# A planned Trainium2 kernel whose scheduler now picks each tile's bank itself: six banks for the first group's first layer, another step pattern

## The chip, the core and the metric

The kernel runs on one core of a Trainium2 chip. The metric is the device time of one execution in microseconds (us), the median of repeated runs; lower is better.

## What is computed

Three layers follow each other: a chunked attention with decays, a block that takes the maximum of three products, and a block with a rational function. Cut to what matters:

```python
# attention: x (4, 8, 768, 32), B, C (4, 8, 768, 16), a (4, 8, 768); chunks of 32 in the reference
L = np.exp(cum[:, :, :, None] - cum[:, :, None, :]) * causal          # cum: cumsum of log(clip(a))
y = ((C @ B^T) * L) @ x + (C @ state) * np.exp(cum)[..., None]
state = decay_full * state + sum_j B_j x_j decay_from_j
x = y.transpose(0, 2, 1, 3).reshape(3072, 256)
# layer 1: d_ff = 768
x = np.maximum(np.maximum(x @ w1, x @ w2), x @ w3) @ w_out            # 256 -> 768 -> 256
# layer 2: d_ff = 2048
h = x @ w_in
P = a[0] + a[1] * h + a[2] * h**2 + a[3] * h**3
Q = 1.0 + abs(b[0]) * abs(h) + abs(b[1]) * h**2
out = (P / (Q + 1e-06)) @ w_out2                                      # 256 -> 2048 -> 256
```

The six weight matrices come as 64-bit floats and are converted on the chip.

## The kernel before

**Tiling.** The sequence is cut into six groups of 128 positions (`NG`), so that one group of all four batches is a tile of 512 columns (`T`). Every tile of work is 128 partitions by 512 columns, and one such tile in PSUM is one bank. All eight banks are in use: G, D, S0 to S3, Y0, Y1.

**Attention of a group**, in two halves of four units each: `s_mm` (L585) makes four products C B in S0 to S3 (L597); for each unit `d_mm` (L603) makes the exponent of the decays in one bank (L610, L612), ScalarE takes its exp (L625), and `m_op` (L627) multiplies it on VectorE with the S bank (L630), which frees that bank. `y_intra` (L642), `y_inter` (L653) and `state` (L677, then L687 and L694 on VectorE) do the rest; `y_out` (L657) copies the result out of Y0 and Y1. Group 0's result is split there into a high and a low part (float32r has too few bits for one product, so every product is three matmuls, L749 to L751: high by high, high by low, low by high). The results of groups 1 to 5 are stored in DRAM (`xt_d`) and loaded again by `x_plan` (L813).

**Weights.** `plan_conv` (L297) converts a piece of 128 x 512 weights: DMA (L323), ScalarE (L327, L330, and the high part L286), VectorE (L328, L331, L334), GpSimd (L339 and the low part L343, two halves each). There are 28 pieces: nine of w1 to w3, three of w_out, eight of w_in, eight of w_out2 (`wo2`). The last eight use SBUF places (L0 to L7) that attention leaves.

**Layer 1** of a group (`gy_plan`, L824): 18 products of six matmuls, drained by ScalarE (L286, w1) and VectorE (L840, the maximum with w2's and w3's), split (L386), then two products of 18 matmuls each with w_out. For group 0 `gy_bank` (L800) gives bank G alone to all 20 tiles (`EARLY`); for later groups G and D by turns.

**Layer 2** (`h_plan`, L875, and `o_plan`, L967): 16 steps per group. A step is a product of six matmuls into S0 or S1, the rational function on ScalarE, VectorE and GpSimd, and two accumulating products with wo2 into S2 and S3. How the numerator and denominator are shared out over the engines is the kind of the step, given by `HV` for groups 0 to 4: H is L922, L924 on ScalarE, L925 and L927 on GpSimd, L928 and L929 on VectorE; A is L932, L933, L943 on ScalarE, L934, L946 on VectorE, L945 on GpSimd; P is L932, L933 on ScalarE, L934, L939, L940 on VectorE and L937 on GpSimd. All kinds go on with L948 and L949 (ScalarE), L950, L953, L955 (VectorE), and the split of the result, L286 (ScalarE) and L961 (GpSimd). The last group has kinds of its own (`HL`) and no split.

**What sets the order.** Nothing is issued as it is written. `Plan.op` records each operation with its engine, an assumed duration, what it reads and writes and a due time (`when`, booked by hand through `book`); `Plan.emit` (L216) lists all operations with `listed`, a list scheduler with the planner's own durations, several times with changed keys, and issues the best order found. In the kernel before a tile's place (bank or SBUF buffer) is fixed when the operation is recorded: `bank("G")`, or `ring`, which hands out its places by turns, and a tile waits for the tile that had its place before:

```python
    def tile(self, place, make):
        t = _Tile(make, self.last.get(place, ()))
        self.last[place] = [t]
        return t
```

Of the kernel before, what the change touches and what calls it, by code (L numbers as in the profile page):

```python
# [34 lines left out]
EARLY = 20  # L35
PAIR = 1
HV, HL = "HAHP", "HHKK"
# [9 lines left out]
class _Tile:  # L47


    def __init__(self, make, prevs=()):  # L50
        self.make, self.prevs, self.t = make, prevs, None
        self.first, self.writers, self.readers, self.closed = None, [], [], False
# [44 lines left out]
class Plan:  # L97

    TAIL = {"pe": 0.22, "act": 0.13, "dve": 0.115, "pool": 0.07}
    SWITCH, FIRST_BYTE, LANDED, FLIGHTS, BEGIN = 0.1, 1.25, 1.35, 8, 0.65
    ROUNDS, LOOK, KEEP = 8, (0.0, 0.1, 0.2), (0.0, 1.5)

    def __init__(self):
        self.ops, self.last = [], {}
# [6 lines left out]
    def op(self, engine, busy, fn, reads=(), writes=(), at=None, behind=(), lock=False, mode="", size=0.0):  # L113
        i = len(self.ops)
        deps, after = set(), {w for t in behind for w in t.writers}
        for t in reads:
            assert t.writers and not t.closed
            deps.update(t.writers)
            t.readers.append(i)
        for t in writes:  # L120
            assert not t.closed
            if t.first is None:
                t.first = i
                for p in t.prevs:
                    p.closed = True
                    deps.update(p.writers + p.readers)
# [4 lines left out]
        self.ops.append(_Op(i, engine, busy, fn, [t for t in writes if t.first == i], deps, after - deps, at,  # L131
                            lock, mode, size))

    def listed(self, key, look, keep):
# [9 lines left out]
        moved, mode, landed, order = 0.0, "", [0.0] * self.FLIGHTS, []  # L144

        def at(j):
            t = self.BEGIN
            for i, _ in self.before[j]:
                if i in ops[j].after:
                    t = max(t, start[i])  # L150
                elif ops[i].engine == ops[j].engine != "dma":
                    t = max(t, start[i] + ops[i].busy)
                else:
                    t = max(t, end[i] + (0.05 if ops[j].engine == "pool" else 0.0))
            return t
# [5 lines left out]
        for _ in range(n):  # L161
            t, e = min((max(free[e], min(ready[j] for j in w)), e) for e, w in wait.items() if w)
# [915 lines left out]
```

## Time and profile before

| | |
|---|---|
| median of 3 runs | 569.52 us (569.35 to 569.66) |
| the profiled execution | 570.01 us, its span 568.2 us |
| TensorE (PE) busy | 546.7 us, 96% of the span |
| PE weight loads (PEld) busy | 411.8 us, 72% |
| VectorE (DVE) busy | 513.7 us, 90% |
| ScalarE (ACT) busy | 433.6 us, 76% |
| GpSimd (POOL) busy | 437.9 us, 77% |
| granted TensorE clock | 1.00 throughout |
| HBM traffic | 33.2 MB, nearly all in the first 140 us |

Matmuls are pipelined: a row of 0.39 us starts 0.23 us after the one before it. A busy share is an average over stages, so the windows by stage, further below, say more than this table. In a wait row the engine on the left sat idle until the one on the right had finished; the numbers are the sum, how often, and the longest.

### The profile page before, as it was taken

To read this page: it belongs to the slowest core of one execution; us is meant where nothing else is said; L and a number is where in the kernel's file an instruction comes from. 1 tells how busy PE (TensorE), PEld (TensorE's weight loads), DVE (VectorE), ACT (ScalarE), POOL (GpSimd) and SP (SyncE) were. 2 spreads that over 40 slices of the span, in tenths; PEclk is the share of its full clock that TensorE was granted. 3 is DMA by queue.
4 is the path that set the end of the run, shared out by engine and by line. 5 is a ranking of instruction groups with operands and counts; after the bars stand their busy time and mean duration, and the time that the engine had idled before them with its cause. 6 is when DMAs were issued, how large, how long until landed. Compare 5 with 4: busy or idle time off the path is not lost.

```text
span 568.2 us, 8235 instructions
## 1 busy us (share of the span) xinstructions
PE 546.7 (96%) x2844; PEld 411.8 (72%) x2854; DVE 513.7 (90%) x782; ACT 433.6 (76%) x756; POOL 437.9 (77%) x403
## 2 busy tenths in 40 slices
PE   9889889998999999999999999999999999999997
PEld 4455555567788888888887788878788888887563
DVE  7999899889999998988888987998889899988996
ACT  5767677779888877877787776868777877688983
POOL 1677677789899878777677685767777999879984
PEclk9999999999999999999999999999999999999999
DMA  7966575353000100001000010000000000001000
GB/s 246 311 208 195 179 246 189 118 204 122 1 0 2 37 2 37 1 0 39 0 1 37 1 37 1 1 37 2 0 1 1 1 37 1 0 1 37 2 0 37
DMA packets 13588, 33.71 MB, mean 59 GB/s; under 512 B 2691, under 2 KB 3435, under 8 KB 13547
## 3 DMA queue, kind: packets, MB, share of 16 engines
q1 hardware_dynamic: 13547, 33.20, 17.7%
q8 instruction: 22, 0.36, 0.3%
q14 instruction: 19, 0.16, 0.1%
HBM read 27.27 MB, written 5.91 MB: 58 GB/s over the span
## 4 chain that ended last, share of the span: by engine, by line
PE 42%; DVE 32%; POOL 12%; ACT 7%; issue 5%; DMA 1%; SPq 0%; POOLq 0%; DVEq 0%; ACTq 0%
PE S L750 6%; PE S L751 6%; PE S L749 6%; PE S L979 4%; PE G L749 4%; DVE X L840 4%; DVE Y L953 4%; PE G L751 3%; PE G L750 3%; DVE A L950 3%; DVE A L955 3%; PE D L749 3%; PE D L751 3%; PE D L750 3%; DVE A L630 2%
## 5 line engine op out<-in xcount | busy, mean ns | idle before, releaser
L961 POOL TENSOR_TENSOR A<-A,A 128x512 fp32r<-128x512 f32 x80 | 106.9, 1337 | 10.6 <-ACT A L286 10.3
L948 ACT ACTIVATE Y<-A,qc 128x512 f32<-128x512 f32 x83 | 57.7, 695 | 45.4 <-POOL A L927 30.0
L950 DVE SCALAR_TENSOR_TENSOR A<-A,Y 128x512 f32<-128x512 f32 x83 | 56.4, 680 | 8.2 <-ACT Y L949 7.9
L386 POOL TENSOR_TENSOR H<-X,H 128x512 fp32r<-128x512 f32 x30 | 41.6, 1388 | 27.4 <-ACT H L286 27.3
L749 PE MATMUL S<-A,L 128*128 128x512 f32 x160 | 62.3, 389 | 0.0
L750 PE MATMUL S<-A,L 128*128 128x512 f32 x160 | 62.3, 389 | 0.0
L751 PE MATMUL S<-A,L 128*128 128x512 f32 x160 | 62.3, 389 | 0.0
L339 POOL TENSOR_TENSOR C<-C,E 128x256 uint32<-128x256 uint32 x56 | 45.4, 825 | 21.8 <-DVE C L334 21.0
L953 DVE SCALAR_TENSOR_TENSOR Y<-A,co,Y 128x512 f32<-128x512 f32 x83 | 62.1, 748 | 0.0
L927 POOL TENSOR_TENSOR A<-A,A 128x512 f32<-128x512 f32 x44 | 57.8, 1314 | 3.6
L955 DVE SCALAR_TENSOR_TENSOR A<-A,Y 128x512 f32<-128x512 f32 x83 | 56.7, 683 | 1.3
L286 ACT ACTIVATE A<-A 128x512 fp32r<-128x512 f32 x80 | 50.4, 630 | 8.8 <-DVE A L955 7.4
L749 PE MATMUL G<-xhi,w_hi 128*128 128x512 f32 x126 | 51.7, 410 | 4.1 <-ACT X L286 2.0
L949 ACT ACTIVATE Y<-Y 128x512 f32<-128x512 f32 x86 | 50.3, 584 | 1.8
L751 PE MATMUL G<-xhi,w_lo 128*128 128x512 f32 x126 | 49.2, 391 | 0.0
L750 PE MATMUL G<-xlo,w_hi 128*128 128x512 f32 x126 | 49.2, 390 | 0.0
L925 POOL TENSOR_SCALAR A<-A,co 128x512 f32<-128x512 f32 x44 | 38.7, 880 | 8.1 <-ACT A L924 8.1
L922 ACT ACTIVATE A<-S,co 128x512 f32<-128x512 f32 x40 | 31.2, 780 | 16.3 <-POOL A L961 16.1
L945 POOL TENSOR_TENSOR A<-A,A 128x512 f32<-128x512 f32 x20 | 26.1, 1307 | 21.6 <-DVE A L934 19.7
L749 PE MATMUL D<-xhi,w_hi 128*128 128x512 f32 x90 | 35.6, 395 | 3.7 <-DVE X L840 3.7
L750 PE MATMUL S<-K,win_hi 128*128 128x512 f32 x96 | 37.5, 390 | 0.4 <-DVE K L386 0.4
L749 PE MATMUL S<-K,win_hi 128*128 128x512 f32 x96 | 37.5, 390 | 0.0
(192 smaller groups left out, 1651.8 us busy)
## 6 DMA issues: line engine op xcount, KB each, us to landing
R<-in_wo_dram SPq DMA_DIRECT2D x11, 512.0 KB
R<-in_w_dram SPq DMA_DIRECT2D x9, 512.0 KB
R<-in_win_dram SPq DMA_DIRECT2D x8, 512.0 KB
L<-in_xn_dram SPq DMA_DIRECT2D x6, 512.0 KB
out_dram<-A SPq DMA_DIRECT2D x12, 256.0 KB
xt_d<-L SPq DMA_DIRECT2D x5, 512.0 KB
L<-xt_d SPq DMA_DIRECT2D x5, 512.0 KB
A<-in_bz_dram SPq DMA_DIRECT2D x6, 256.0 KB
```

What stands on the lines that cost most here:

```text
L286: act.activation(out=o, in_=i, func=AF.Copy)
L339: op("pool", 0.7, lambda k=k: pool.tensor_tensor(out=a.t[:, k], in0=a.t[:, k], in1=e.t[:, k], op=ALU.add), [e], [a])
L749: pe.matmul(dst, wh, hi, start=first, stop=False)
L750: pe.matmul(dst, wh, lo, start=False, stop=False)
L751: pe.matmul(dst, wl, hi, start=False, stop=last)
L927: pop(1.26, lambda: pool.tensor_tensor(out=f(v), in0=f(t1), in1=f(v), op=ALU.mult), [t1], [v])
L948: aop(0.6, lambda: act.activation(out=f(r), in_=f(v), func=AF.Ln, bias=qc), [v], [r])
L949: aop(0.49, lambda: act.activation(out=f(r), in_=f(r), func=AF.Exp, scale=-1.0), [], [r])
L950: dop(0.6, lambda: dve.scalar_tensor_tensor(out=f(v), in0=f(v), scalar=QC, in1=f(r), op0=ALU.add, op1=ALU.mult), [r], [v])
L953: dop(0.67, lambda: dve.scalar_tensor_tensor(out=f(r), in0=f(w), scalar=c(0), in1=f(r), op0=ALU.add, op1=ALU.mult), [w], [r])
L955: dop(0.6, lambda: dve.scalar_tensor_tensor(out=f(w), in0=f(v), scalar=2.0, in1=f(r), op0=ALU.subtract, op1=ALU.mult), [v, r], [w])
L961: pop(1.26, lambda: pool.tensor_tensor(out=f(lo), in0=f(w), in1=f(hi).bitcast(F32), op=ALU.subtract), [w, hi], [lo])
```

## The change

Places are no longer given out when an operation is recorded. A tile carries a list of places that it may have, and `listed` gives it, at the moment at which its first writer is issued, the first of them that is free, or the one that will be free soonest (`spot`). Operations of one kind keep their order among themselves (`turn`). A tile marked `final` waits for all tiles that could have its place. On top of that:

- Decays (`d_mm`) may have D or G in all groups (before: G and D by turns in group 0, then D alone). Layer 1 of group 0 may have any of G, D, S0 to S3.
- The fourth step of `HV` is of kind H in place of P.
- Group 1's attention result stays in SBUF (`x1`): one store and one load of 512 KB go.
- In the last group the product of a step may have G, D, S0, S1 and its reciprocal Y0, Y1 (before: G, D, and S0, S1 or Y0, Y1).
- Products of layer 2 may not be issued before the last four L630 of attention have begun; `state` follows its group's exp. The planner's price of a change of TensorE's mode is 0.12 in place of 0.10, and decays count as a mode.

```diff
-EARLY = 20
-PAIR = 1
-HV, HL = "HAHP", "HHKK"
+SBANKS, DBANKS, FIRST_BANKS, GBANKS = (), ("D", "G"), ("G", "D", "S0", "S1", "S2", "S3"), ("G", "D")
+LAST, LAST_R = ("G", "D", "S0", "S1"), ("Y0", "Y1")
+HV, HL = "HAHH", "HHKK"
...
-    def tile(self, place, make):
-        t = _Tile(make, self.last.get(place, ()))
-        self.last[place] = [t]
+    def tile(self, places, make, final=False, kind=None):
+        t = _Tile(make, places, kind)
+        if final:
+            t.prevs = [p for p in self.tiles if places[0] in p.places] + self.fixed.get(places[0], [])
+        self.tiles.append(t)
         return t
...
+        for k in [turn] * bool(turn) + [t.kind for t in writes if t.first is None and len(t.places) > 1]:
+            if k in self.turns:
+                after.add(self.turns[k])
+            self.turns[k] = i
...
+        def spot(i):
+            t, got = ready[i], []
+            for x in ops[i].first:
+                best = None
+                for p in x.places:
+                    if not open_.get(p) and p not in got:
+                        u = behind(users.get(p, ()), i, 0.0)
+                        if best is None or u < best[0] - 1e-9:
+                            best = u, p
+                        if u <= t:
+                            break
+                if best is None:
+                    return None
+                t = max(t, best[0])
+                got.append(best[1])
+            return t, got
...
-        t = bank("G" if g < PAIR and d_n[0] % 2 else "D")
+        t = bank(*DBANKS, kind="d")
...
-        if g:
+        if g == 1:
+            x1.append(xo)
+        elif g:
             xt_t[g] = mark()
             load(lambda: xt_d[g], lambda: xo.t, [xt_t[g]], [xo], kb=524)
...
     def gy_bank(g):
-        banks[0] += 1
-        if g:
-            return pg()
-        return bank("G") if banks[0] <= EARLY else late()
+        return bank(*(GBANKS if g else FIRST_BANKS), kind="g")
...
-        t = pg() if last else ph()
+        t = bank(*(LAST if last else ("S0", "S1")))
...
-           when["h", s] + (0.5 * 6 * MM if c0 else 0))
+           when["h", s] + (0.5 * 6 * MM if c0 else 0), behind=[m_t[u] for u in range(NG * NU - 4, NG * NU)], turn="h")
...
-        r = ph() if last and (k + (c0 > 0)) % 3 else pr()
+        r = bank(*(LAST_R if last else ("Y0", "Y1")))
```

Three places show how the instructions stand now. Lines of the changed kernel are other ones: L703 is L630 of before, L909 is L840, L460 is L386, L406, L409 and L412 are L328, L331 and L334, L715 is L642, L824 to L826 are L749 to L751.

**VectorE in the middle of attention, around group 0's layer 1.** X0 and X1 are the running maxima, the second operand is the bank that is drained, S0 to S3 in L630 are attention's products. Before:

```order
L630 TENSOR_TENSOR A16_538<-S0_469,A10_533 128x512
L579 TENSOR_TENSOR A3_482<-A3_482,sm_94 128x512
L328 TENSOR_SCALAR C1_548<-C1_548 128x512
L840 TENSOR_TENSOR X0_453<-X0_453,G_540 128x512
L331 TENSOR_SCALAR C1_548<-C1_548 128x512
L334 SCALAR_TENSOR_TENSOR C1_548<-R2_362,C1_548 128x512
L630 TENSOR_TENSOR A17_585<-S1_470,A11_563 128x512
L386 TENSOR_TENSOR H6_599<-X0_453,H0_574 128x512
```

Now:

```order
L909 TENSOR_TENSOR X0_519<-X0_519,S0_618 128x512
L909 TENSOR_TENSOR X0_519<-X0_519,G_632 128x512
L703 TENSOR_TENSOR A15_699<-S3_555,A13_585 128x512
L909 TENSOR_TENSOR X1_671<-X1_671,S2_661 128x512
L460 TENSOR_TENSOR H6_708<-X0_519,H0_701 128x512
L406 TENSOR_SCALAR C1_705<-C1_705 128x512
L409 TENSOR_SCALAR C1_705<-C1_705 128x512
L412 SCALAR_TENSOR_TENSOR C1_705<-R1_544,C1_705 128x512
L909 TENSOR_TENSOR X1_671<-X1_671,S1_677 128x512
```

Before, one maximum out of G stands between attention's multiplications; now layer 1 of group 0 stands in one piece, out of six banks, between the fifth and the sixth half-group of attention, and no L630 stands among the following rows.

**VectorE at the end of attention**, from the last two L630 on. Before:

```order
L630 TENSOR_TENSOR A_1610<-S_1526,A_1595 128x512
L630 TENSOR_TENSOR A_1622<-S_1527,A_1614 128x512
L328 TENSOR_SCALAR C_1632<-C_1632 128x512
L331 TENSOR_SCALAR C_1632<-C_1632 128x512
L334 SCALAR_TENSOR_TENSOR C_1632<-R_1488,C_1632 128x512
L386 TENSOR_TENSOR K_1660<-G,K_1642 128x512
L386 TENSOR_TENSOR xlo_1676<-L_1612,xhi_1664 128x512
L386 TENSOR_TENSOR xlo_1682<-L_1612,xhi_1666 128x512
```

Now:

```order
L412 SCALAR_TENSOR_TENSOR C_1583<-R_1410,C_1583 128x512
L703 TENSOR_TENSOR A_1648<-S_1559,A_1596 128x512
L406 TENSOR_SCALAR C_1646<-C_1646 128x512
L409 TENSOR_SCALAR C_1646<-C_1646 128x512
L909 TENSOR_TENSOR X_1636<-X_1636,G 128x512
L412 SCALAR_TENSOR_TENSOR C_1646<-R_1476,C_1646 128x512
L997 TENSOR_TENSOR A_1683<-S_1658,A_1683 128x512
```

The splits of layer 1's result (K) and of group 1's input (xlo) are no longer behind attention; the first maximum of group 1 stands there.

**TensorE at the same place.** Y is attention's result, H by wo the last product of group 0's layer 1, K by win the first product of layer 2, xhi by w the first products of group 1's layer 1. Before:

```order
L749 MATMUL G<-H_1327,wo_hi 128x512
L750 MATMUL G<-H_1329,wo_hi 128x512
L751 MATMUL G<-H_1327,wo_lo 128x512
L642 MATMUL Y_1503<-A_1570,L_1250 32x128 x2
L642 MATMUL Y_1503<-A_1588,L_1250 32x128 x2
```

Now:

```order
L826 MATMUL D<-xhi_940,w_lo 128x512
L715 MATMUL Y_1529<-A_1599,L_1353 32x128 x2
L715 MATMUL Y_1529<-A_1611,L_1353 32x128 x2
L715 MATMUL Y_1529<-A_1599,L_1353 32x128 x2
L715 MATMUL Y_1529<-A_1611,L_1353 32x128 x2
L824 MATMUL G<-xhi_919,w_hi 128x512
```

Group 0's layer 1 is done long before, and the first two products of group 1 (12 matmuls, one on either side of the first of the two last L715 steps) stand where group 0's last ones stood.

## Rows read from the trace of the kernel before

**Rows 1.** Busy us (instructions) by stretch: length, PE, PEld, DVE, ACT, POOL, clock, DMA, GB/s.
```profile
0.00:12.00 12.00, 10.72 (x43) 5.34 (x43) 8.57 (x18) 7.07 (x12) 1.16 (x5) 1.00 0.75 233
0.00:122.70 122.70, 110.75 (x959) 65.08 (x970) 111.23 (x184) 87.57 (x155) 81.03 (x99) 1.00 0.64 210
122.70:214.40 91.70, 88.80 (x415) 72.08 (x414) 88.59 (x130) 76.57 (x134) 82.70 (x75) 1.00 0.11 39
214.40:520.00 305.60, 302.93 (x1333) 249.28 (x1332) 271.38 (x401) 234.21 (x404) 237.79 (x196) 1.00 0.03 11
```

**Rows 2.** Waits of PE, 122.7 to 520 us: sum us, times, longest us.
```profile
PE D L749 <- DVE X L840: 3.7, 5, 1.0
PE G L749 <- ACT X L286: 1.5, 1, 1.5
PE S L750 <- DVE K L386: 0.4, 1, 0.4
```

**Rows 3.** Waits of DVE, 12 to 122.7 us.
```profile
DVE A L630 <- ACT A L625: 2.2, 6, 0.6
DVE C L328 <- ACT C L327: 2.1, 3, 0.7
```

**Rows 4.** Groups of DVE, first 123 us: count, busy us, mean ns, idle before.
```profile
L334 DVE SCALAR_TENSOR_TENSOR C<-R,C 128x512 uint32<-128x512 uint32 x23 | 20.5, 892 | 0.7
L328 DVE TENSOR_SCALAR C<-C 128x512 f32<-128x512 f32 x23 | 13.0, 564 | 2.8 <-ACT C L327 2.7
L331 DVE TENSOR_SCALAR C<-C 128x512 uint32<-128x512 uint32 x23 | 12.7, 551 | 0.7
L386 DVE TENSOR_TENSOR xlo<-L,xhi 128x512 fp32r<-128x512 f32 x2 | 1.3, 670 | 0.0
```

**Rows 5.** Timeline at attention's end, DVE then PE: start us, us, instruction.
```profile
121.18 1.48 DVE L630 TENSOR_TENSOR A<-S,A 128x512 f32<-128x512 f32 x2
...
122.69 0.39 PE L751 MATMUL G<-H,wo_lo 128*128 128x512 f32 x1
122.92 0.39 PE L749 MATMUL G<-H,wo_hi 128*128 128x512 f32 x1
```

**Rows 6.** Timeline of PE: the S products of one half-group.
```profile
87.42 1.15 PE L597 MATMUL S<-cz,A 32*128 32x256 f32 x16
```

**Rows 7.** Timeline of DVE in a P step.
```profile
317.64 1.79 DVE L940 SCALAR_TENSOR_TENSOR A<-A,co,A 128x512 f32<-128x512 f32 x1
```

**Rows 8.** Groups of DVE, whole span: steps P (L934, L940) and H (L929).
```profile
L934 DVE SCALAR_TENSOR_TENSOR A<-A,co,A 128x512 f32<-128x512 f32 x40 | 35.2, 881 | 1.7 <-ACT A L932 1.7
L929 DVE SCALAR_TENSOR_TENSOR A<-A,co,S 128x512 f32<-128x512 f32 x40 | 29.8, 746 | 2.5 <-ACT A L924 1.3
L940 DVE SCALAR_TENSOR_TENSOR A<-A,co,A 128x512 f32<-128x512 f32 x20 | 23.2, 1162 | 0.5
```

**Rows 9.** Groups of POOL, 122.7 to 214.4 us.
```profile
L961 POOL TENSOR_TENSOR A<-A,A 128x512 fp32r<-128x512 f32 x16 | 21.7, 1355 | 2.8 <-ACT A L286 2.8
L343 POOL TENSOR_TENSOR L<-C,L 128x256 fp32r<-128x256 f32 x13 | 13.0, 1011 | 1.1 <-ACT L L286 1.1
L927 POOL TENSOR_TENSOR A<-A,A 128x512 f32<-128x512 f32 x9 | 12.4, 1381 | 0.7
L386 POOL TENSOR_TENSOR H<-X,H 128x512 fp32r<-128x512 f32 x7 | 10.0, 1428 | 2.3 <-ACT H L286 2.3
L339 POOL TENSOR_TENSOR C<-C,E 128x256 uint32<-128x256 uint32 x11 | 9.5, 876 | 0.0
L925 POOL TENSOR_SCALAR A<-A,co 128x512 f32<-128x512 f32 x10 | 8.9, 892 | 0.0
L945 POOL TENSOR_TENSOR A<-A,A 128x512 f32<-128x512 f32 x5 | 6.7, 1337 | 1.3 <-ACT A L286 0.7 <-DVE A L934 0.6
L937 POOL TENSOR_SCALAR A<-A,co 128x512 f32<-128x512 f32 x4 | 3.3, 819 | 0.7 <-ACT A L932 0.7
```

More of the change, by code (lines that the diff above doesn't have):

```diff
@@ L130, in op @@
         after.discard(i)
-        self.ops.append(_Op(i, engine, busy, fn, [t for t in writes if t.first == i], deps, after - deps, at,
-                            lock, mode, size))
+        self.ops.append(_Op(i, engine, busy, fn, [t for t in writes if t.first == i and t.places], deps,
+                            after - deps, at, lock, mode, size))
     def listed(self, key, look, keep):
@@ L144, in listed, with behind, at @@
         moved, mode, landed, order = 0.0, "", [0.0] * self.FLIGHTS, []
-        def at(j):
-            t = self.BEGIN
[L148 to L155, printed above, removed]
+        users, open_ = dict(self.of_fixed), dict(self.open_fixed)
+        place, had = {}, {}
+        def behind(js, i, t):
+            e = ops[i].engine
+            for j in js:
+                if ops[j].engine == e != "dma":
+                    t = max(t, start[j] + ops[j].busy)
+                else:
+                    t = max(t, end[j] + (0.05 if e == "pool" else 0.0))
+            return t
+        def at(i):
+            t = self.BEGIN
+            for j, _ in self.before[i]:
+                if j in ops[i].after:
+                    t = max(t, start[j])
+            return behind([j for j, _ in self.before[i] if j not in ops[i].after], i, t)
+        def spot(i):
[14 more added lines that the diff above has]
+            return t, got
         for j in range(n):
@@ L166, in listed @@
             order.append(j)
-            t, o = max(t, ready[j]), ops[j]
+            t, o = max(t, can[j]), ops[j]
+            if o.first:
+                got = spot(j)[1]
+                had[j] = [i for p in got for i in users.get(p, ())]
+                for x, p in zip(o.first, got):
+                    place[x] = p
+                    users[p], open_[p] = x.writers + x.readers, len(set(x.writers + x.readers))
             if e == "dma":
@@ L188, in listed @@
                     wait[ops[i].engine].append(i)
-        return order, start, max(end)
+        self.place = place
+        return order, start, max(end), had
     def placed(self, key, before, then):
@@ L218, in emit @@
         ops, n = self.ops, len(self.ops)
[L219 removed]
+        self.before, self.then, self.touch = [[] for _ in range(n)], [[] for _ in range(n)], [[] for _ in range(n)]
         for o in ops:
@@ L233, in emit @@
                 for keep in self.KEEP:
-                    order, start, end = self.listed(key, look, keep)
+                    order, start, end, had = self.listed(key, look, keep)
                     if best is None or end < best[0]:
-                        best = end, order, start
-            start = best[2]
-            mirror = self.placed([-(start[i] + span[i]) for i in range(n)], back, self.before)
+                        best = end, order, start, had, self.place
+            start, had = best[2:4]
+            before, then = [list(b) for b in self.before], [list(b) for b in self.then]
+            for j, js in had.items():
+                for i in js:
+                    l = ops[i].lag(ops[j])
+                    before[j].append((i, l))
+                    then[i].append((j, l))
+            back = [[(j, l - span[i] + span[j]) for j, l in then[i]] for i in range(n)]
+            mirror = self.placed([-(start[i] + span[i]) for i in range(n)], back, before)
             far = max(mirror[i] + span[i] for i in range(n))
@@ L587, in s_mm @@
         g, a = divmod(k, 2)
-        ts = [bank(f"S{h}") for h in range(4)]
+        ts = [bank(*(SBANKS or (f"S{h}",)), kind=f"s{h}") for h in range(4)]
         for h in range(4):
```

145 lines of the change are left out of this document (84 added, 61 removed).

## Prediction

> **What bounds the kernel now.** I read the windows first, then the waits of the engine that each window names, then groups and the timeline at the seams. The windows [rows 1] cut the span in three. Up to 122.7 us, where attention's last multiplication ends [rows 5], VectorE is busy 111.23 us of 122.7 and TensorE 110.75; but TensorE works there on small shapes and waits for banks, and its weight loads take only 65.08, while VectorE is 8.57 busy in the first 12.0 us and 102.66 in the other 110.7. So VectorE is the bound: 11.5 us of idle, 3.4 of it at the start. From 122.7 to 214.4 (the last low half of the last weight piece) three engines are nearly full: TensorE 88.80, VectorE 88.59, GpSimd 82.70 of 91.7. From 214.4 on TensorE alone is the bound (302.93 of 305.6; VectorE 271.38, GpSimd 237.79). Behind 122.7 TensorE runs one matmul each 0.23 us (the two starts in [rows 5], 122.69 and 122.92), and all its waits up to 520 us make 5.6 us [rows 2]. So the time is: when attention ends, plus what TensorE has left by then, plus these waits. A change can win in three ways only: end attention earlier, put more matmuls ahead of its end, or take waits away.
>
> **Term 1, attention's end: -2.2.** VectorE's work ahead of the last L630 hardly changes in amount. By the order, one weight piece less stands ahead of it (564 + 551 + 892 ns = 2.0 us [rows 4]) and three more splits L386 do (3 x 0.67 = 2.0 [rows 4]). What can go is idle time. Two kinds of wait make up the larger part [rows 3]: L630 for the exponent of ScalarE, 2.2 us in six waits, and a weight piece for ScalarE's L327, 2.1 in three. The first hangs on the decays: behind group 0 all of them pass through bank D alone, so exponent and next product take turns. With D and G by turns the next product stands ready while ScalarE empties the other bank. I take all 2.2. The second has nothing to do with banks, and I leave it. The bounds: at best only the first 3.4 us of idle stay, 11.5 - 3.4 = 8.1, say -8.0; at worst a loss, which is rival D.
>
> **Term 2, TensorE's stock at that moment: -3.6.** Before, four matmuls of group 0's layer 1 stand behind the last L630: 4 x 0.23 = 0.9 us. Now group 0's layer 1 is long done, and 12 matmuls of group 1's layer 1 have moved ahead of attention's last products: 12 x 0.227 = 2.7. TensorE had the room for them: its weight loads are 65.08 of 122.7. Together 3.6 less to do after attention. The bounds are 0, if those 12 only delay the last products, and -3.6.
>
> **Term 3, waits at the seam: -1.9.** A product waited 0.4 us for the split of K on VectorE, and one 1.5 for ScalarE's drain of G [rows 2]. Both stand behind attention before; now K and xlo are split earlier, and group 1 begins with products that wait for nothing. Bounds: 0 and -1.9.
>
> **Term 4, waits in layer 2: -2.7.** Five times a first matmul into D waited for a maximum on VectorE, 3.7 us in all, the longest 1.0 [rows 2]. One is at the seam and I keep it, at 1.0. The other four come behind the fourth step, of kind P, in which L940 needs two SBUF operands and took up to 1.79 us [rows 7] against a mean of 1162 ns [rows 8]: the maximum queued behind it is late, so the bank is. Kind H has no L940 and drains its bank in L929, at 746 ns against the 881 of L934 [rows 8]. So 3.7 - 1.0 = 2.7 go. Bounds: 0 and -2.7. What is late next is GpSimd: a step P gave it L937 alone (819 ns), a step H gives it L925 and L927 (892 + 1381 ns), 1.45 us more per step [rows 9].
>
> L940's row shows more than a wait: its instances differ by a microsecond with the same shape. The Trainium skill, "SBUF — State Buffer", section "Who interferes with whom", gives a reason: VectorE's second SBUF input and GpSimd's reads share a port pair that one of them holds for a whole instruction while the other is blocked. By that rule P to H would give VectorE back, with 1162 against 746 ns and 881 against 746, about 0.55 us in each of 20 steps, 11 us. I count only the 2.7 us for which TensorE waited [rows 2], since behind 214.4 us VectorE has 34 us to spare [rows 1].
>
> **Term 5, given back: +3.0.** GpSimd in the middle stretch. Counted in the order from attention's end to the last low half of wo2, it has 73 operations before (11 L339, 12 L343, 7 L386, 9 L925, 9 L927, 4 L937, 5 L945, 16 L961), by the means of [rows 9] 83.8 us against 82.70 measured, and now 76 (14, 14, 6, 12, 12, none, 4, 14): 86.6 us. One half, 1.0, belongs to a product that comes later; if half of its 9.0 us of idle (91.7 - 82.70) stays, it needs 86.6 - 1.0 + 4.5 = 90.1. TensorE has 374 matmuls to do by then, 374 x 0.227 = 84.9, and the kept wait of 1.0. So the low halves are late by 90.1 - 85.9 = 4.2. I take off 1.2 for the time in which GpSimd itself was blocked by the VectorE operations that P has and H has not, a guess from the scatter of [rows 8], and keep +3.0. Bounds: 0 (no idle left) and 90.1 + 4.5 - 85.9 = +8.7 (all idle stays).
>
> **Costed at nothing.** Group 1's store and load go from SP's queue: DMA is at 0.11 in the middle stretch and no wait in [rows 2] names one. The first weight piece now stands ahead of group 0's attention input on that queue; cover: eight decay products that need no such input, until about 16 us; without it, 524 KB at 233 GB/s [rows 1] = 2.2 us. `turn` and `behind` only order what already stands in this order. GpSimd's 1.45 us in each of the other 16 steps P, 23 us, have some 68 us of idle to lie in, 305.6 - 237.79 [rows 1]. The last group's product may take four banks and its reciprocal only Y0 and Y1: the same number of tiles, no term.
>
> **Sum.** -2.2 - 3.6 - 1.9 - 2.7 + 3.0 = -7.4. The profiled execution is 570.01, so 562.6 on its scale; the median is 0.5 below it, so **562.1 us**.
>
> **The rivals.** A is the forecast: 0.50.
>
> B, GpSimd is the bound in the first layer 2 group and keeps all its idle time: term 5 is +8.7, the sum -1.7, 567.8 us. For it: 82.70 busy there with an idle that three different releasers end [rows 9], and three operations more. Against: it works from lists that are longer than what waits for them. Chance 0.16.
>
> C, banks were what held VectorE up: two kinds of decay banks and six for layer 1 leave only its first 3.4 us of idle (term 1 is -8.0), conversions are then early enough that nothing is given back. -8.0 - 3.6 - 1.9 - 2.7 = -16.2: 553.3 us. Against: the waits on L327 [rows 3] are no bank waits. Chance 0.12.
>
> D, slower. Before, layer 1 of group 0 is spread through attention and fills both engines whenever a half-group turns over. Now it is done in one piece, behind the fifth half-group, and the last six halves have less to fill with. In each, VectorE would idle during the S products (1.15 us [rows 6]) and one conversion wait (0.7 [rows 3]): 1.85 x 6 = 11.1 us, and term 1's 2.2 isn't won: -7.4 + 2.2 + 11.1 = +5.9, 575.4 us. Without term 1 the other terms make -5.2, so it decides from 5.2 / 6 = 0.87 us of new idle per half. For it: the second place in the order, with no maximum near the last L630 until group 1's first. Against: weight pieces (23 L334 up to there [rows 4]) still stand between, and group 1's first layer is at hand. Chance 0.16.
>
> The rest, 0.06, lies within 0.2%: B with a little of D. That the change does not do what it says is out: the order shows maxima out of S0 to S3.
>
> **Numbers.** What a measurement can tell from no change is 0.2%, 1.1 us. Faster by more: A, B and C, 0.78. Same: 0.06. Slower: D, 0.16. The range must hold 8 in 10. Down it reaches to C, 553.0. Up it takes in B and the milder part of D, up to 1.2 us of new idle per half (1.2 x 6 - 5.2 = +2.0): 571.5. A's own range is 558 to 566, from the bounds of terms 1 to 4 at half their size each way.
>
> **What would show it.** Right: the last L630 ends near 120.5; no wait of TensorE at the seam longer than 1.0; no wait of L749 for VectorE's maximum behind 214 us; L630 waits little for ScalarE; the last low half of wo2 is late by a few microseconds, and a product of wo2 waits for it. Wrong: attention's end later than 122.7 with VectorE idle between halves (D); GpSimd waits named behind products all over the first layer 2 group (B); attention's end before 117 (C). A gain with attention's end unmoved and the waits as before would mean that the time went where I read nothing.

## The result, and the profile after

The changed kernel takes 564.08 us (median of 4 runs, 563.55 to 564.51), the kernel before beside it 569.59 us: the ratio is 0.990, with a 95% interval of 0.9883 to 0.9917, so 5.5 us faster. The profiled execution of it took 563.55 us, the lowest of the four, at a span of 561.4 us; against the profiled one of before (span 568.2) that is 6.8 us less, and it is this difference that the traces explain.

The windows of the changed kernel, cut at the same events as [rows 1]: attention's last multiplication, the last low half of the last weight piece, and the start of the last group's steps.

```profile
0.00:12.00 12.00, 10.42 (x29) 4.97 (x30) 9.25 (x21) 7.48 (x14) 1.16 (x5) 1.00 0.73 215
0.00:118.40 118.40, 109.17 (x989) 69.10 (x1002) 108.71 (x185) 88.04 (x158) 80.13 (x95) 1.00 0.64 211
118.40:203.40 85.00, 82.47 (x369) 65.70 (x368) 81.41 (x115) 69.70 (x120) 80.31 (x76) 1.00 0.11 38
203.40:512.00 308.60, 305.71 (x1341) 250.80 (x1340) 263.58 (x396) 241.47 (x414) 253.77 (x217) 1.00 0.03 11
```

Attention ends 4.3 us earlier (118.4 for 122.7), and the middle stretch is 6.7 us shorter (85.0 for 91.7) with VectorE at 81.41 for 88.59 and GpSimd at 80.31 for 82.70: VectorE is about as full as before (96% for 97%), GpSimd fuller (94% for 90%). The last low half comes 11.0 us earlier, not later. The timeline of VectorE and then of TensorE at attention's end, which answers to [rows 5]:

```profile
116.51 0.68 DVE L703 TENSOR_TENSOR A<-S,A 128x512 f32<-128x512 f32 x1
117.71 0.68 DVE L703 TENSOR_TENSOR A<-S,A 128x512 f32<-128x512 f32 x1
```

```profile
118.07 0.39 PE L826 MATMUL G<-xhi,w_lo 128*128 128x512 f32 x1
118.30 0.40 PE L824 MATMUL S<-K,win_hi 128*128 128x512 f32 x1
122.50 0.65 PE L715 MATMUL Y<-A,L 128*32 128x128 f32 x16
123.07 0.50 PE L824 MATMUL G<-xhi,w_hi 128*128 128x512 f32 x1
```

Behind the last L703 TensorE has products of group 1 and of layer 2 at hand, and issues attention's last product only at 122.50. The waits of VectorE from 12 us to attention's end (to [rows 3]), and of TensorE from there to 512 us (to [rows 2]):

```profile
DVE K L460 <- ACT K L363: 1.1, 1, 1.1
DVE D L762 <- PE D L752: 1.0, 1, 1.0
DVE C L406 <- ACT C L405: 0.9, 1, 0.9
DVE A L703 <- PE S L671: 0.9, 1, 0.9
```

```profile
PE S L824 <- DVE A L998: 2.7, 5, 1.2
PE D L824 <- ACT X L363: 1.1, 1, 1.1
PE S L824 <- DVE A L1015: 1.0, 2, 0.7
PE D L824 <- DVE X L909: 0.3, 1, 0.3
```

No L703 waits for the exponent of the decays any more (2.2 us before). But TensorE's waits behind attention are 5.1 us where they were 5.6: those for the maximum went but for 0.3, and 3.7 came for L998 and L1015, each the last reader of a step's bank. VectorE's groups up to 118.4 us (to [rows 4]; the last row is the one of before that belongs to the row ahead of it):

```profile
L412 DVE SCALAR_TENSOR_TENSOR C<-R,C 128x512 uint32<-128x512 uint32 x22 | 19.8, 898 | 0.7
L406 DVE TENSOR_SCALAR C<-C 128x512 f32<-128x512 f32 x23 | 11.6, 503 | 1.4 <-ACT C L405 1.2
L460 DVE TENSOR_TENSOR xlo<-L,xhi 128x512 fp32r<-128x512 f32 x4 | 3.8, 946 | 0.0
L460 DVE TENSOR_TENSOR H<-X,H 128x512 fp32r<-128x512 f32 x6 | 4.5, 754 | 0.1
L386 DVE TENSOR_TENSOR H<-X,H 128x512 fp32r<-128x512 f32 x6 | 6.6, 1096 | 1.6 <-ACT H L286 1.4
```

One weight piece less and more splits, as the order said; VectorE's busy time up to there is still 2.5 us less, because single operations are shorter: the splits of layer 1 at 754 ns where they took 1096, L406 at 503 where L328 took 564. Its idle time is 9.7 us for 11.5, so the 4.3 us are 2.5 of shorter work and 1.8 of idle time.

**A split of the difference.** Attention's last product L715 (L642 before) cuts every trace of this study at one point of the work. The head is the time at which the next product starts, plus 0.227 us for each matmul that the order has left then; the part behind is the time from there to the end of the last matmul, less 0.227 us for each matmul left. Before: the next product starts at 124.70 with 1808 matmuls (of 128x512, as the order has them) left. Changed: at 123.07 with 1778. So the head is 1.63 + 30 x 0.227 = 8.4 us better, the part behind it (439.7 - 410.4 = 29.3 us over the matmuls' own time before, 434.4 - 403.6 = 30.8 now) 1.5 worse, the end 0.1 worse: -8.4 + 1.5 + 0.1 = -6.8 us. All runs in this split, in us against the profiled execution of before:

| run | head | behind | end | sum | ratio of the medians to before |
|---|---|---|---|---|---|
| the change | -8.4 | +1.5 | +0.1 | -6.8 | 0.990 |
| before, H A H H alone | +3.2 | -2.1 | -0.1 | +1.0 | 0.9973 |
| changed, H A H P | -7.9 | +8.3 | +0.2 | +0.6 | 1.0013 |
| P in the first group alone | -7.5 | +3.1 | +0.2 | -4.3 | 0.9951 |
| P in groups 1 to 4 alone | -8.1 | +0.5 | +0.2 | -7.5 | 0.987 |
| H in all steps of groups 1 to 4 | -7.6 | +2.2 | +0.2 | -5.2 | 0.9929 |
| first layer 1 in G alone | -10.7 | +13.8 | +0.2 | +3.3 | 1.0042 |
| decays in D alone | +1.8 | -2.3 | +0.6 | +0.1 | 1.0011 |
| last group's banks as before | -8.0 | +9.4 | +0.2 | +1.5 | 1.0026 |
| another price of a mode | -7.2 | +1.4 | +0.6 | -5.3 | 0.9917 |
| VectorE's load in the first group | -7.7 | +5.5 | +0.2 | -2.0 | 0.9998 |
| VectorE's load in groups 1 to 4 | -7.9 | +18.8 | +0.2 | +11.1 | 1.0187 |
| GpSimd's load in the first group | -8.3 | +5.9 | +0.2 | -2.1 | 0.9991 |

The sums are of one execution each, the ratios of the medians. One per cent is 5.7 us. The profiled execution of before lies 0.4 us over its median, that of the change 0.5 under its own. In some executions of a kernel TensorE's mean granted clock is a little lower (0.997 for 1.00, say) and the time one or two microseconds longer; those at 0.999 or 1.00 alone have a median of 569.5 us with H A H P, 566.0 with P in the first group, 568.3 with VectorE's load and 568.1 with GpSimd's load there, 569.2 before.

### The profile page after: what moved, and what is told of

Read it like the earlier page. It is cut to its first block, busy times and chain, and to the rows that moved or that the text cites. A ratio compares the mean times of both kernels' runs of the same rounds, so it can differ in the third digit from the quotient of the medians.

```text
span 561.4 us, 8364 instructions
## 1 busy us (share of the span) xinstructions
PE 542.2 (97%) x2842; PEld 411.9 (73%) x2854; DVE 496.6 (88%) x762; ACT 435.4 (78%) x756; POOL 452.1 (81%) x423
## 4 chain that ended last, share of the span: by engine, by line
DVE 38%; PE 23%; POOL 17%; ACT 12%; issue 8%; DMA 1%; SPq 1%; POOLq 0%; DVEq 0%; ACTq 0%
DVE Y L1022 6%; DVE A L1019 5%; DVE A L1024 5%; POOL A L996 5%; DVE X L909 4%; POOL A L994 4%; PE S L1048 3%; ACT Y L1017 3%; DVE A L998 3%; POOL A L1030 3%; DVE A L997 3%; PE S L824 2%; PE S L826 2%; PE S L825 2%; ACT Y L1018 2%
## 5 line engine op out<-in xcount | busy, mean ns | idle before, releaser
L1017 ACT ACTIVATE Y<-A,qc 128x512 f32<-128x512 f32 (+1 forms) x89 | 61.4, 690 | 40.2 <-POOL A L996 30.9
L1019 DVE SCALAR_TENSOR_TENSOR A<-A,Y 128x512 f32<-128x512 f32 (+1 forms) x89 | 60.4, 679 | 31.9 <-ACT Y L1018 30.9
L996 POOL TENSOR_TENSOR A<-A,A 128x512 f32<-128x512 f32 x64 | 84.8, 1325 | 4.5
L1022 DVE SCALAR_TENSOR_TENSOR Y<-A,co,Y 128x512 f32<-128x512 f32 (+1 forms) x89 | 66.5, 747 | 0.4
L994 POOL TENSOR_SCALAR A<-A,co 128x512 f32<-128x512 f32 x64 | 51.6, 806 | 14.6 <-ACT A L993 14.3
L363 ACT ACTIVATE A<-A 128x512 fp32r<-128x512 f32 x80 | 50.6, 632 | 15.6 <-DVE A L1024 11.2
L1024 DVE SCALAR_TENSOR_TENSOR A<-A,Y 128x512 f32<-128x512 f32 (+1 forms) x89 | 60.7, 682 | 2.2
L824 PE MATMUL S<-A,L 128*128 128x512 f32 x160 | 62.3, 389 | 0.0
L826 PE MATMUL S<-A,L 128*128 128x512 f32 x160 | 62.2, 389 | 0.0
L1018 ACT ACTIVATE Y<-Y 128x512 f32<-128x512 f32 (+1 forms) x97 | 56.2, 580 | 2.5
L991 ACT ACTIVATE A<-S,co 128x512 f32<-128x512 f32 x60 | 46.8, 780 | 12.5 <-POOL A L1030 11.3
L460 POOL TENSOR_TENSOR H<-X,H 128x512 fp32r<-128x512 f32 x30 | 40.8, 1359 | 16.7 <-ACT H L363 16.5
L998 DVE SCALAR_TENSOR_TENSOR A<-A,co,S 128x512 f32<-128x512 f32 x60 | 44.8, 747 | 1.9
L997 DVE TENSOR_TENSOR A<-S,A 128x512 f32<-128x512 f32 x60 | 41.0, 684 | 1.9 <-ACT A L991 1.9
L824 PE MATMUL S<-K,win_hi 128*128 128x512 f32 x96 | 38.0, 395 | 2.1 <-DVE A L998 1.2
L824 PE MATMUL D<-xhi,w_hi 128*128 128x512 f32 x94 | 36.9, 393 | 1.4 <-ACT X L363 1.1
L1014 POOL TENSOR_TENSOR A<-A,A 128x512 f32<-128x512 f32 x20 | 25.9, 1296 | 14.9 <-DVE A L1003 14.9
L826 PE MATMUL S<-K,win_lo 128*128 128x512 f32 x96 | 37.4, 389 | 0.0
```

The costliest lines, as they stand in the source:

```text
L824: pe.matmul(dst, wh, hi, start=first, stop=False)
L826: pe.matmul(dst, wl, hi, start=False, stop=last)
L994: pop(0.74, lambda: pool.tensor_scalar(out=f(t1), in0=f(v), scalar1=c(5), scalar2=c(4), op0=ALU.mult, op1=ALU.add), [v], [t1])
L996: pop(1.26, lambda: pool.tensor_tensor(out=f(v), in0=f(t1), in1=f(v), op=ALU.mult), [t1], [v])
L998: dop(0.67, lambda: dve.scalar_tensor_tensor(out=f(w), in0=f(w), scalar=c(1), in1=f(t), op0=ALU.add, op1=ALU.mult), [t], [w])
L1017: aop(0.6, lambda: act.activation(out=f(r), in_=f(v), func=AF.Ln, bias=qc), [v], [r])
```

## The experiments

Two theories stood at the start: B, that the free choice of banks gains, and P, that the step pattern does.

**The pattern alone, in the kernel before.**

```diff
-HV, HL = "HAHP", "HHKK"
+HV, HL = "HAHH", "HHKK"
```

> The kernel before with the step pattern H A H H alone; places stay fixed. Theory B (the gain is the banks'; the pattern only trades waits): the four waits of the D product for VectorE's maximum go, 2.7 us, but products then wait for L929 or for the low halves instead, as they do in the changed kernel; 568 to 571 us, within 0.3% of before. Theory P (the pattern carries the gain, VectorE being freed of L940 in 20 steps): at least 3 us less, 566.5 us or lower, with TensorE's waits behind attention falling from 5.6 us to under 3. Both: attention's end stays within 1 us of 122.7.

567.19 us, ratio 0.9973 (0.9953 to 0.9992): 1.5 us faster. Behind attention it is 2.1 us better than before. Its head can't be read from this profile, since TensorE's granted clock was 0.91 in one stretch of attention and 0.83 in another (shares of 2.4 GHz, so partly at 1.2):

```profile
20.00:40.00 20.00, 17.53 (x177) 10.46 (x166) 18.50 (x31) 13.62 (x26) 14.17 (x17) 0.91 0.87 290
60.00:80.00 20.00, 16.53 (x130) 9.32 (x130) 14.86 (x23) 13.44 (x24) 13.77 (x18) 0.83 0.58 181
```

B holds so far by the ratio (the time itself lies between the two theories): the pattern by itself is not the gain. TensorE's waits behind attention are 3.0 us here, for 5.6 before.

**Everything but the pattern.**

```diff
-HV, HL = "HAHH", "HHKK"
+HV, HL = "HAHP", "HHKK"
```

> The changed kernel with the old step pattern H A H P; the order is the same up to attention's end and changes only behind it. Theory B: 562.5 to 565.5 us, TensorE's waits behind attention between 4 and 7 us, part of them again for the maximum. Theory P: 567 us or more. Term 5 of the prediction (GpSimd gives 3 us back in the first layer 2 group) would make it about 3 us faster there and 2.7 slower later; both at once would leave 564 as well, but then the last low half of wo2 comes at least 2 us earlier than 203.4.

569.99 us, ratio 1.0013 (1.0000 to 1.0026). So the banks by themselves gain nothing either: B falls, and P with it, as P alone gave 1.5. The head is there, 7.9 us of it, and 8.3 are lost behind it (a lower clock for 3.4 us has a part in them, last section). The middle stretch, up to the last low half of wo2, and TensorE's waits from attention's end to 519 us:

```profile
118.90:207.80 88.90, 85.40 (x371) 66.67 (x369) 85.56 (x119) 69.41 (x121) 78.98 (x75) 0.98 0.10 36
```

```profile
PE S L824 <- DVE A L998: 3.8, 6, 1.3
PE S L824 <- DVE A L1015: 2.5, 1, 2.5
PE G L824 <- DVE X L909: 1.1, 3, 0.6
```

The stretch is 3.9 us longer than in the changed kernel and VectorE has 4.2 us more in it; GpSimd has 1.3 less, and its low halves come 4.4 us later all the same. TensorE's head start ends in waits for VectorE. That is a third theory, V: the banks bring TensorE's work forward, and it is worth something only as far as VectorE follows.

**Bank G alone for layer 1 of the first group.**

```diff
-FIRST_BANKS = ("G", "D", "S0", "S1", "S2", "S3")
+FIRST_BANKS = ("G",)
```

(The four lists stand in one assignment; the diff shows the one that is changed, here and in the next run.)

> The changed kernel with bank G alone for layer 1 of the first group; decays keep D and G. Theory B1 (six banks bring attention's end forward): attention's end back to 120.5 to 123, 566 to 569 us. Theory B2 (the two banks of the decays bring it): attention's end at 118 to 119.5, 563.5 to 565.5 us, no wait of L703 for ScalarE's exponent over 0.5 us in sum. A third case: G now is shared by decays and layer 1 and blocks both; later than 123, over 570 us.

571.59 us, ratio 1.0042 (1.0026 to 1.0059). None of the three cases: attention's end is not late but early, at 84.8 us, because the scheduler does attention first and layer 1 of the first group behind it, one bank at a time:

```profile
PE G L824 <- DVE X L909: 9.0, 11, 1.0
PE G L824 <- ACT X L363: 3.0, 4, 1.0
```

So with the decays in two banks attention alone needs no more than 85 us, and what the six banks give is that layer 1 goes without 12 us of waits. It also shows that attention's end by itself is no measure of the head.

**Bank D alone for the decays.**

```diff
-DBANKS = ("D", "G")
+DBANKS = ("D",)
```

> The changed kernel with bank D alone for the decays; layer 1 of the first group keeps its six banks. Theory B2: the wait of L703 for the exponent is back, 2 us or more, attention's end at 120.5 or later, 566 us or more. Theory B1: attention's end within 1 us of 118.4, 563.5 to 565.5 us. Before had D alone from the second group on and G and D by turns in the first, so the first group's decays get one bank less than they had: up to 1 us more than before there.

570.07 us, ratio 1.0011 (0.9998 to 1.0024). The wait of L703 for the exponent is back, and attention's end is at 133.3. VectorE's wait, and TensorE's in the whole span:

```profile
DVE A L703 <- ACT A L698: 4.0, 4, 2.3
```

```profile
PE D L681 <- ACT A L698: 6.9, 9, 1.0
```

The head is lost entirely, 10.2 us of it (+1.8 for -8.4). So without the decays' second bank there is no head, as theory B2 said. With attention late, the part behind it is 2.3 us better than before, as in the run with the pattern alone: what the change is worth behind attention depends on when attention ends.

**Another price of a change of mode in the planner.**

```diff
-    SWITCH = 0.12
+    SWITCH = 0.1
```

> The changed kernel with the planner's price of a change of mode at 0.10 in place of 0.12: the same banks, pattern and rules, but a new order from the first half-group on. Theory J (banks and pattern gain together, whatever the order): 562.5 to 565.5 us, ratio to before 0.988 to 0.993. Theory L (the gain is one lucky order among many, each some us apart): 567 us or more, ratio 0.996 or more.

564.74 us, ratio 0.9917 (0.9903 to 0.9931), with another order from the first half-group on. Theory J holds: the gain does not hang on this one order. The other order is about 1 us away. With one such pair it is not known how far orders scatter, and differences of one to three microseconds between runs that were planned anew carry this doubt. As 0.10 is the price that the kernel before has, this part of the change is worth about 1 us at most, and the two intervals overlap.

**VectorE's load put back into the first group, in the same order.**

```diff
-        dop(0.6, lambda: dve.scalar_tensor_tensor(...), [v, r], [w])
+        dop(0.6, lambda: [dve.scalar_tensor_tensor(...) for _ in range(3 if k % 4 == 3 and g == 0 else 1)], [v, r], [w])
```

> The changed kernel, its order kept to the instruction, with L1024 issued three times in every fourth step of the first layer 2 group: 2 x 0.68 = 1.37 us more of VectorE a step, as much as kind P has over H by the rows (0.88 + 0.69 + 1.16 less 0.69 + 0.75 = 1.29), four steps, 5.5 us in all. Theory V (VectorE sets the first layer 2 group, 81.4 of 85.0 us busy): 3 to 5.5 us slower than the changed kernel, ratio to before 0.995 to 1.000. Theory G (GpSimd sets it, as in term 5 of the prediction): under 1.5 us slower, ratio below 0.993.

568.84 us, ratio 0.9998 (0.9985 to 1.0011): the whole gain is gone, for 5.5 us of load (4.2 us of it in the executions at full clock, 568.3 for 564.1). The last low half of wo2 comes 3.8 us later (207.3), and TensorE waits 4.0 us for L998 where it waited 2.7. Theory V holds by its range. But the load also makes the step that carries it longer, so a kept order cannot tell a full engine from a late step; the planned runs below do.

**The same load in groups 1 to 4** (the condition is `0 < g < NG - 1`).

> As the run with VectorE's load in the first group, but in the second to fifth: 16 steps, 22 us more of VectorE, where it has 308.6 - 263.6 = 45 us idle. Theory V: at most 2 us slower, ratio to before 0.990 to 0.9935, since TensorE's products have two banks to run ahead in. Theory T (every delay behind a fourth step holds up a bank, term 4 of the prediction, 0.7 us each): 16 x 0.17 = 2.7 us and more, ratio 0.995 or higher.

579.88 us, ratio 1.0187 (1.0166 to 1.0209): 16 us slower for 22 us of load. V falls here, and T holds by its letter only, at six times its size. All five executions have a mean clock under 1.00 (0.993 to 0.997); in the profiled one TensorE ran twice for 3.4 us at 0.50, by an estimate some 3 us of the 16 (last section). VectorE still has idle time, and TensorE still waits for it. From 204 us on, VectorE's two longest waits and TensorE's:

```profile
DVE A L1019 <- ACT Y L1018: 26.9, 20, 2.3
DVE A L1015 <- POOL A L1014: 7.8, 6, 1.5
```

```profile
PE D L824 <- DVE X L909: 5.7, 4, 2.5
PE S L824 <- DVE A L998: 5.1, 7, 2.2
```

The idle time lies in front of L1019 and L1015, which wait for the ScalarE and GpSimd operations of their own step; a load that comes at another place of the fixed order doesn't fall into it.

**GpSimd's load in the first group, in the same order** (the L994 of the same four steps three times).

```diff
-            pop(0.74, lambda: pool.tensor_scalar(...), [v], [t1])
+            pop(0.74, lambda: [pool.tensor_scalar(...) for _ in range(3 if k % 4 == 3 and g == 0 else 1)], [v], [t1])
```

> The changed kernel, its order kept, with L994 issued three times in every fourth step of the first layer 2 group: 2 x 0.86 = 1.7 us more of GpSimd a step, 6.9 us in all. Theory G: 4 to 7 us slower, ratio to before 0.997 or more, with products of wo2 waiting for low halves. Theory V: under 2 us slower, ratio below 0.9935, as GpSimd has 85.0 - 80.3 = 4.7 us idle there and its low halves come early.

568.33 us, ratio 0.9991 (0.9976 to 1.0006): 5.2 us for 6.9 us of load. So in this order GpSimd has as little room as VectorE there, theory G holds, and V is too narrow. The middle stretch (GpSimd is the fifth busy time), and TensorE's wait for the low half of a step's result, which the changed kernel has not:

```profile
118.50:208.60 90.10, 85.26 (x378) 66.92 (x377) 83.30 (x117) 69.72 (x121) 86.73 (x84) 1.00 0.10 36
```

```profile
PE S L825 <- POOL A L1030: 1.0, 1, 1.0
```

**P in the first group alone, planned anew.**

```diff
-        kind = HL[k % len(HL)] if last else HV[k % len(HV)]
+        kind = HL[k % len(HL)] if last else (HV if g else "HAHP")[k % len(HV)]
```

> The changed kernel with kind P back in the fourth steps of the first group alone, planned anew behind attention. Theory F (VectorE is full in the first layer 2 group, so that four steps x 1.3 us there decide): ratio to before 0.997 to 1.002, 567.5 to 570 us, nearly all that H A H P in all groups cost (1.0013). Theory E (each of the 20 steps costs the same 0.3 us): 1.3 us over the changed kernel, ratio 0.990 to 0.994.

566.95 us, ratio 0.9951 (0.9933 to 0.9969), between the two theories: the first group's four steps are worth 0.5% (0.9951 against 0.990), 2.9 us, of the 6.4 that the pattern is worth in the changed kernel (at full clock about 2 of 5.4). VectorE and the stretch again, 86.27 of 89.2 us:

```profile
119.30:208.50 89.20, 84.45 (x373) 65.79 (x372) 86.27 (x120) 70.69 (x124) 81.06 (x76) 1.00 0.11 36
```

**P in groups 1 to 4 alone, planned anew** (`("HAHP" if g else HV)`).

> The changed kernel with kind P back in the fourth steps of the second to fifth group, the first kept at H A H H. Theory F: the planner finds room for VectorE there (45 us idle), ratio to before 0.989 to 0.9935, at most 2 us over the changed kernel. Theory E: 5 us over it, ratio 0.997 or more. The run with three L1024 in a kept order, 16 us slower, would then show what an order that doesn't know of a load costs, not what the load costs.

562.54 us, ratio 0.987 (0.9849 to 0.9891): no slower than the changed kernel, and the fastest kernel of the study. VectorE is at 279.75 of 308.3 us behind the first group, 91%, and TensorE loses nothing by it:

```profile
118.70:203.70 85.00, 82.55 (x370) 65.81 (x369) 81.03 (x115) 69.71 (x121) 80.23 (x77) 1.00 0.11 38
203.70:512.00 308.30, 307.18 (x1345) 251.31 (x1344) 279.75 (x412) 239.75 (x415) 240.38 (x203) 1.00 0.03 11
```

By this the 16 us of the kept order were in the main the price of an order that doesn't know of the load: P there adds 16 us of VectorE (279.75 for 263.58) and takes 13 off GpSimd (240.38 for 253.77), and a planner that knows it finds the room. But the later groups are not free in every case: with P in the first group too, the later P costs another 0.6% (1.0013 against 0.9951). Whether this kernel is really faster than the changed one stays open: the intervals touch (0.9891 and 0.9883), and the two were not run side by side.

**The last group's banks.**

```diff
-LAST, LAST_R = ("G", "D", "S0", "S1"), ("Y0", "Y1")
+LAST, LAST_R = ("G", "D"), ("S0", "S1", "Y0", "Y1")
```

> The changed kernel with the banks of the last group as before: products in G and D, reciprocals in S0, S1, Y0, Y1. The order changes in the last group alone. The prediction gave this no term: ratio 0.989 to 0.992. If the four banks of the products do something, it is in the last 45 us, where the changed kernel's gaps of TensorE make 11.2 us against 12.9: up to 1.7 us slower, ratio 0.993.

571.08 us, ratio 1.0026 (1.0011 to 1.0041): 7.2 us slower than the changed kernel, where at most 1.7 was expected. The order is that of the changed kernel up to the last group. In the last group the reciprocals now sit in S0 and S1 too, VectorE waits for them, and TensorE, which has two banks for its products, for VectorE. VectorE's waits from 500 us on, where the changed kernel has 1.6 and 0.2 us for L1019, and TensorE's from 510 us on:

```profile
DVE H L1019 <- ACT S L1018: 3.3, 3, 1.5
DVE A L1019 <- ACT S L1018: 2.3, 3, 1.1
DVE H L997 <- ACT H L993: 1.9, 1, 1.9
```

```profile
PE S L1048 <- DVE A L1024: 1.5, 2, 1.2
PE S L1048 <- DVE H L1024: 1.0, 1, 1.0
```

The lists are those of the kernel before, but there the places went by fixed turns and the order was another; before's own last group is not behind the changed one: from 500 us to its last matmul TensorE is idle for 0.1 us before, 0.5 in the changed kernel and 4.4 here (the 12.9 against 11.2 us of the expectation do not come out of the traces). In the profiled execution some 1.7 us more, by an estimate, are a lower clock in the last group (last section); the loss doesn't rest on it, as an execution at a mean clock of 1.00 took 571.06 us.

**H in all steps of groups 1 to 4** (`("HHHH" if g else HV)`).

> The changed kernel with kind H in all steps of the second to fifth group: VectorE 16 x (0.96 + 0.75 - 0.69 - 0.75) = 4.3 us less there, GpSimd 16 x (0.81 + 1.33 - 1.30) = 13.4 us more, of some 50 us idle. If VectorE's load still costs time behind the first group, up to 2 us faster than the changed kernel, ratio 0.986 to 0.990; if GpSimd's is as dear, up to 5 us slower, ratio up to 1.000; from the few waits left behind 204 us, 4.9 us in all, I expect no more than 0.3% either way.

565.12 us, ratio 0.9929 (0.9904 to 0.9954): within 0.3% of the changed kernel, as expected. Less of VectorE there is worth nothing that shows, in line with the run with P in groups 1 to 4; the 13.4 us more of GpSimd that go with it were not tried by themselves.

## Why the prediction was right, and where it was not

The forecast was 562.1 us and the range 553.0 to 571.5; the time is 564.1, faster as forecast. The sum held better than its terms, and that is in part luck: the terms for the head made -5.8 and it measures -8.4, those behind it -1.9 - 2.7 + 3.0 = -1.6 and that part measures +1.5, so an error of 2.6 us one way stands against one of 3.1 the other way.

**Terms 1 and 2 (attention's end -2.2, the stock -3.6): right in kind, too small.** Attention's end moved 4.3 us, and the other 4.1 are matmuls ahead, near the 3.6 of the stock. (12 matmuls were counted ahead of attention's last products; by the timeline 30 are, 18 of them started behind the last L703 or as it ended.) Term 1 was read too narrowly: I counted VectorE's 2.2 us of waits for the exponent [rows 3], which went entirely, but not that VectorE's operations would take 2.5 us less up to there, nor that TensorE too waits for the one bank; VectorE's idle time fell by 1.8 us, less than the 2.2, as other waits came. The run with decays in D alone has a head 10.2 us worse than the change.

**Terms 3 and 4 (waits that go, -1.9 and -2.7): too large.** Where attention is not early (the pattern alone, and decays in D alone) the part behind it is 2.1 and 2.3 us better, not 4.6. With the pattern alone term 4 came: TensorE's waits there are 3.0 us for 5.6. In the changed kernel it did not. The step that failed is "So 3.7 - 1.0 = 2.7 go": the waits for the maximum went, and [rows 2] has waits for L998 and L1015 in their place, 3.7 us in the changed kernel. A product here needs a free bank, and when VectorE is late the next product waits for whatever reads that bank last.

**Term 5 (given back, +3.0): the size near, the engine half wrong.** With the head, the part behind is +1.5; without it, -2.1 and -2.3: some 3.7 us are given back, if the two runs with a late attention may be taken as the measure (a late attention may also let VectorE and GpSimd get ahead; that was not separated). But not through late low halves: they are early, and no product of wo2 waits for one. The sentence that failed is "it needs 86.6 - 1.0 + 4.5 = 90.1": the idle time came as assumed, 4.7 us, but GpSimd was busy for 80.31 only. Its 14 low halves alone took 3.3 us less (the row below, 774 ns against 1011 in [rows 9]). The 1.2 us taken off for blocking are shown by no run.

```profile
L421 POOL TENSOR_TENSOR L<-C,L 128x256 fp32r<-128x256 f32 x14 | 10.8, 774 | 0.7 <-ACT L L363 0.7
```

[rows 1] had VectorE at 88.59 of the same 91.7 us, and I priced only the engine that the change loads. The stretch follows both: 85.0 us with VectorE at 81.4, 88.9 with 85.6 (H A H P), 89.2 with 86.3 (P in the first group), 90.1 with GpSimd at 86.7.

**What was missed altogether: that the parts multiply.** By the terms, the change without the pattern should have won 7.4 - 2.7 + 3.0 = 7.7 us without a give-back, or 4.7 with it; it lost 0.7 (1.0013). The pattern alone won 1.5. Together they win 5.5, so 5.5 + 0.7 - 1.5 = 4.7 us belong to neither, against about 1 us between two orders. The reading that fits the stretches above: the banks bring TensorE's work forward, H takes four times 1.3 us from VectorE in the one stretch where VectorE is full, and each is worth little while the other engine holds the end. The first group has 2.9 us of the pattern's 6.4, shown by the planned run, and the load put back into it in a kept order takes all 5.6 (4.2 at full clock). How the remaining 3.5 arise in the later groups, where P costs nothing once the first group has H, was not separated: a VectorE that is late from the first group on is what the two runs suggest.

**Costed at nothing.** "The same number of tiles, no term" for the last group failed by 7.2 us against that choice of lists, though by nothing that shows against the kernel before. Store and load of group 1's result, the order of the first weight piece, `turn` and `behind` were not tried by themselves; no wait of TensorE or VectorE in the traces names a transfer there.

**The rule of the Trainium skill** ("SBUF — State Buffer", section "Who interferes with whom") was taken for 11 us from P to H, the waits for 2.7. The measured worth is 6.4 us in the changed kernel, 1.5 in the one before and none in the later groups alone. The 11 us are only what two operations of P took over 746 ns; a step P also has one operation more, and by the rows' means H takes 1.3 us a step less (0.88 + 0.69 + 1.16 against 0.69 + 0.75). VectorE's busy time in the whole span fell by 16.2 us with the pattern alone (513.7 to 497.5) and by 23.4 from H A H P to the changed kernel (520.0 to 496.6). So what is set free is known from VectorE's busy time, and the place tells what it is worth. That VectorE operations with two SBUF operands vary in length agrees with it (P's L1009 took 970 ns on average in the run with P in groups 1 to 4, L940 1162 in [rows 8]); no run here separated the blocking itself.

**The rivals.** B (GpSimd keeps all its idle time, 567.8) did not come: its low halves are 11.0 us earlier. C (553.3) did not: VectorE is still idle for 9.7 us up to attention's end. D (halves with nothing to fill, 575.4) did not: no L703 waits over 0.9 us. It had the wrong place: layer 1 in one piece costs nothing as long as it has its banks, and costs 8.1 us (1.0042) with one.

## What to carry to other kernels

When two engines are both full in a stretch, price a change by both, and price its parts together: here the banks gave TensorE a head start and the step pattern gave VectorE the time to follow, and each alone was worth 1.5 us or nothing. Idle time of an engine with a fixed order is room only for a load that the order knows of: 22 us of VectorE cost 16 us in a kept order, and 16 us of VectorE cost nothing when planned. A wait that a change removes is often renamed: ask what the waiting engine would be waiting for next before the sum counts it as won.

## What was not expected of the hardware

A wait of TensorE can be dear twice, but it is not so each time. In the run with H A H P it had nothing to do for 2.5 us while it waited for L1015. It went on at 148.25 us, and behind 148.8 its granted clock was 0.50 in place of 1.00, which is 1.2 in place of 2.4 GHz, though it was busy throughout by then. The same came in the run on the last group's banks, behind two shorter pauses. The windows of the first, then of the second (TensorE's busy time is the first number behind the length, the clock the third from the end), and two timeline rows of the second, of one shape:

```profile
146.00:148.00 2.00, 0.00 (x0) 0.00 (x0) 2.00 (x2) 0.57 (x1) 2.00 (x2) 1.00 0.00 0
148.00:150.00 2.00, 1.75 (x5) 1.46 (x6) 1.97 (x4) 0.00 (x0) 1.92 (x3) 0.71 0.69 238
150.00:152.00 2.00, 2.00 (x6) 1.54 (x5) 1.96 (x4) 1.19 (x3) 0.23 (x1) 0.50 0.06 25
```

```profile
550.00:552.00 2.00, 1.11 (x7) 0.77 (x6) 1.97 (x4) 1.97 (x4) 1.92 (x3) 1.00 0.00 0
552.00:553.00 1.00, 0.04 (x1) 0.04 (x1) 0.97 (x3) 1.00 (x3) 0.97 (x1) 1.00 0.00 0
554.00:555.00 1.00, 1.00 (x3) 0.35 (x2) 0.96 (x3) 1.00 (x3) 1.00 (x1) 0.50 0.00 0
```

```profile
552.96 3.09 PE L1048 MATMUL S<-H,R 128*128 128x512 f32 x4 [1.01 <-DVE H L1024]
558.91 1.88 PE L1048 MATMUL S<-H,C 128*128 128x512 f32 x4
```

Four such matmuls took 3.09 us, most of it at the lower clock, and 1.88 at the higher. The stretch at 0.50 lasted 3.4 us in both, so it cost some 1.7 us by an estimate (half of it), on top of the wait ahead of it.

But the run with P in the first group alone has the same wait of 2.50 us at the same place of the work, and behind it the clock stays at 1.00:

```profile
148.60 0.50 PE L824 MATMUL S<-K,win_hi 128*128 128x512 f32 x1 [2.50 <-DVE A L1015]
```

```profile
148.00:150.00 2.00, 1.40 (x6) 1.18 (x7) 1.97 (x4) 0.00 (x0) 1.92 (x3) 1.00 0.53 174
150.00:152.00 2.00, 1.65 (x9) 1.03 (x7) 1.96 (x4) 1.65 (x3) 1.04 (x2) 1.00 0.22 88
```

That is the profiled execution of this kernel, 565.70 us at a mean clock of 1.00. Of its eight executions six have a mean clock of 0.997 or less, and they took 566.3 to 568.2 us. In all the traces of this study TensorE has five pauses of over 2 us between matmuls: the clock fell behind four of them (2.2 to 2.5 us, in the runs with H A H P, with the pattern alone, and twice with VectorE's load in groups 1 to 4), and not behind this one. It also fell twice behind shorter pauses (the run on the last group's banks, and the pattern alone at 28 us). The waits of [rows 2], up to 1.5 us, were followed by nothing of the kind: the windows of [rows 1] are at 1.00. So a pause alone doesn't settle whether the clock falls, and what does was not tried.
